# A channel-product weight scheme moved one batch earlier, with filled waits in the first attention: a three-layer mixer on one Trainium2 core

## The chip, the cores and the metric

The kernel runs on one core of one Trainium2 chip. The metric is the time of one execution on the device in microseconds; the profile is one such execution with every instruction recorded. The engines are PE (TensorE: matmuls, with PEld for its weight loads), DVE (VectorE), ACT (ScalarE), POOL (GpSimd) and SP (SyncE, which here only issues DMAs).

## What is computed

Eight batches of 576 tokens with 512 features pass through a chunked attention (8 heads of 64, chunks of 64 tokens), a token and channel mixer with ReLU, and a gated unit with a spatial product:

```python
# attention, per batch, head and chunk of 64 tokens
p = exp(s - max(s)); attn = p / (sum(p) + 1e-9)      # s = q k^T / 8
x = attn @ v                                          # (8, 576, 512)
# mixer
u = x + (relu(x^T @ w_tok1) @ w_tok2)^T               # 576 -> 256 -> 576
x = u + relu(u @ w_ch1) @ w_ch2                       # 512 -> 1536 -> 512
# gated unit
h = relu(x @ w_in)                                    # 512 -> 1024, halves g and v
v_n = (v - mean(v)) / sqrt(var(v) + 1e-6)
out = (g * (w_spatial @ v_n + b)) @ w_out             # 512 -> 512
```

All inputs and the output are float32; q and k are scaled so that the scores spread widely.

## The kernel before

Each float32 operand is held as two float16 parts (hi and lo), and a product is three float16 matmuls (hi·hi, hi·lo, lo·hi), 288 or 512 columns wide. The work runs batch by batch. In a batch PE goes through the first channel product (`ch1`), the second (`ch2`), the first token product of the next batch (`tok1`), the gate products (`gate_v`, `gate`), the second token product of the next batch (`tok2`), the spatial product (`gated`), and the output products (`proj`), four or five of which are left for the next batch. Batches are counted from 0.

From some batch on the two channel products are formed from seven products of quarter blocks in place of eight (`ch1_fast` at line 750, `ch2_fast` at line 834). They need sums of weight blocks, which `sum_steps` (line 665) makes once: `join` adds the two parts on DVE (L683) and, for each block that is used as it is, issues DMAs to a buffer in HBM (L687, L691); `first` and `second` are four sums on POOL (L695, L696, L699, L700); `high` splits on ACT (L703), `low` on DVE (L706), and its DMAs (L708, L713) store the result. Before, the first channel product is formed so from batch 2 on (`FIRST_FAST = 2`) and the second from batch 3 on (`FIRST_FULL = 3`): the sums for the first are made in batch 1 and those for the second in batch 2, while batch 2 runs the full `ch2` (L921, 288 matmuls). `ch1_fast(full)` stores its result either as it is (`store`, when the second product is still full) or as the seven block sums that `ch2_fast` needs (`sums_of`).

Attention for batch b+1 runs in batch b, in tiles of 128 tokens. Batches 0 and 1 have `wide_steps` (line 343, float32 matmuls on PE); batch 0's stands alone at the start of the program, in the order of the list `FIRST_ORDER` (sc score, sh maximum, ex exponentials, nm division, tn transposes on PE, tu their copy, at the product with v, oh and ol the split), with the first weight splits (U, L, H, O) between. From the attention for batch 2 on, `at_steps` (line 225) has each tile's steps at the places `TIMES` (line 426): load of q and k at 0, score at 10.9, `p_lo` on POOL at 17.2, `p_turn` (a transposing DMA, L281) at 18, `attend` (L298) at 23.7, `x_turn` (the next transposing DMA, L320) at 27.2.

What sets the order. PE's instructions stand in the order in which the program is written. `pump` (line 467) advances a clock by each matmul's columns, and `tick` calls what is due by it: attention steps, weight sums, and operations that `after` put off by one of `LAGS`. `PACES` scales the attention's clock by stage, `SPAN` its length. From batch 2 on ACT, DVE, POOL and SP are in written order too (`manual_schedule`, `exact`); in batches 0 and 1 a scheduler chooses their order. `bank()` hands out four PSUM tiles in turn; a product waits for its tile to be emptied.

## Time and profile before

| what | value |
|---|---|
| median of 3 runs | 1127.51 us (1127.5 to 1128.74) |
| the profiled execution's own time | 1132.01 us |
| its span, first to last instruction | 1130.2 us |
| PE busy | 1084.3 us (96%) |
| DVE, ACT, POOL busy | 773.1, 515.2, 436.6 us |
| granted TensorE clock, mean | 0.994 of full |

The span begins with the first instruction. A busy PE is not PE at its peak: matmuls overlap each other, so their rate is read from the starts of following groups. A view by stretch of time shows how much of a stretch each engine works, and a timeline shows the idle time before a row and what ended it.

### The profile page before, as it was taken

To read this page: it belongs to the slowest core of one execution; us is meant where nothing else is said; L and a number is where in the kernel's file an instruction comes from. 1 tells how busy PE (TensorE), PEld (TensorE's weight loads), DVE (VectorE), ACT (ScalarE), POOL (GpSimd) and SP (SyncE) were. 2 spreads that over 40 slices of the span, in tenths; PEclk is the share of its full clock that TensorE was granted. 3 is DMA by queue.
4 is the path that set the end of the run, shared out by engine and by line. 5 is a ranking of instruction groups with operands and counts; after the bars stand their busy time and mean duration, and the time that the engine had idled before them with its cause. 6 is when DMAs were issued, how large, how long until landed. Compare 5 with 4: busy or idle time off the path is not lost.

```text
span 1130.2 us, 26065 instructions
## 1 busy us (share of the span) xinstructions
PE 1084.3 (96%) x10860; PEld 771.6 (68%) x10860; DVE 773.1 (68%) x1301; ACT 515.2 (46%) x1040; POOL 436.6 (39%) x416
## 2 busy tenths in 40 slices
PE   5898999999999899999999999999999999999998
PEld 4577757776676675776667666777767767677765
DVE  4899977665455677878577676877768774577342
ACT  6455543434335445456254652556344652346131
POOL 0000032534244464656235551375435551255221
PEclk9899999999999999999999999999999999999999
DMA  9478620454027675255931678245931666024401
GB/s 325 138 236 269 198 75 20 127 146 113 6 54 217 160 135 119 54 158 163 249 76 47 175 181 189 51 117 164 238 89 36 172 166 190 1 66 147 134 1 47
DMA packets 147270, 148.31 MB, mean 131 GB/s; under 512 B 95824, under 2 KB 108112, under 8 KB 144848
## 3 DMA queue, kind: packets, MB, share of 16 engines
q1 hardware_dynamic: 147152, 146.64, 47.9%
q8 instruction: 85, 1.39, 0.5%
q14 instruction: 33, 0.27, 0.1%
HBM read 112.00 MB, written 20.45 MB: 117 GB/s over the span
## 4 chain that ended last, share of the span: by engine, by line
PE 72%; DVE 13%; ACT 5%; DMA 3%; POOL 3%; issue 3%; SPq 0%; DVEq 0%; ACTq 0%; POOLq 0%
PE mp L735 22%; PE mp L499 21%; PE mp L921 8%; PE mp L947 7%; PE mp L1035 7%; PE mp L522 3%; DVE gb L155 1%; PE mp L246 1%; ACT inw L377 1%; DMA pT<-p 1%; PE mp L298 1%; DVE gb L159 1%; DMA x<-xht 1%; DVE c L803 1%; DVE hb L624 1%
## 5 line engine op out<-in xcount | busy, mean ns | idle before, releaser
L735 PEld LDWEIGHTS <-c1w 128*128 128x128 f16 x2772 | 269.0, 98 | 80.2 <-issue 7.6
L735 PE MATMUL mp<-xb,c1w 128*128 128x288 f16 x864 | 129.1, 286 | 4.2 <-DVE vn L797 2.6
L921 PE MATMUL mp<-hb,c2w 128*128 128x288 f16 x864 | 111.6, 289 | 0.0
L499 PE MATMUL mp<-spw,vn 128*128 128x288 f16 x896 | 111.2, 286 | 0.1
L499 PEld LDWEIGHTS <-vn 128*128 128x128 f16 x896 | 87.6, 98 | 22.6 <-issue 0.3
L499 PE MATMUL mp<-xb,inw 128*128 128x288 f16 x768 | 100.2, 286 | 0.1
L921 PEld LDWEIGHTS <-c2w 128*128 128x128 f16 x864 | 83.8, 99 | 22.1
L1035 PE MATMUL mp<-otw,gb 128*128 128x512 f16 x432 | 98.1, 379 | 0.0
L735 PE MATMUL mp<-hb,c1w 128*128 128x288 f16 x630 | 90.4, 286 | 2.0 <-ACT vn L863 1.9
L499 PEld LDWEIGHTS <-inw 128*128 128x128 f16 x768 | 74.3, 98 | 23.5 <-issue 0.3
L735 PE MATMUL mp<-c2w,c1w 128*128 128x288 f16 x630 | 89.7, 286 | 0.0
L947 PE MATMUL mp<-inw,xb 128*128 128x512 f16 x384 | 87.3, 379 | 0.8 <-DVE x L416 0.8
L499 PE MATMUL mp<-xb,c1w 128*128 128x288 f16 x576 | 73.4, 286 | 4.9 <-DVE xb L583 2.5
L1035 PEld LDWEIGHTS <-gb 128*128 128x128 f16 x432 | 42.3, 98 | 45.4
L1023 POOL TENSOR_TENSOR gb<-gt,gb 128x576 f16<-128x576 f32 x31 | 43.3, 1402 | 69.6 <-ACT gb L1022 69.6
L499 PEld LDWEIGHTS <-c1w 128*128 128x128 f16 x576 | 55.7, 98 | 20.1 <-issue 5.0
L947 PEld LDWEIGHTS <-xb 128*128 128x128 f16 x384 | 37.4, 98 | 43.3 <-issue 1.0
L970 POOL TENSOR_TENSOR y<-z,mhalf 128x1 f32<-128x1 f32 (+1 forms) x40 | 25.7, 643 | 104.3 <-DVE z L969 104.3
L735 PE MATMUL mp<-c1w 128*128 128x288 f16 x432 | 64.7, 286 | 0.0
L981 POOL TENSOR_TENSOR vn<-vt,vn 128x512 f16<-128x512 f32 x32 | 37.8, 1181 | 57.3 <-ACT vn L980 57.3
L695 POOL TENSOR_TENSOR xs<-xs 128x128 f32<-128x128 f32 x12 | 8.7, 724 | 115.4 <-DVE xs L683 115.4
L499 PE MATMUL mp<-t2w,hb 128*128 128x288 f16 x384 | 49.1, 286 | 1.8 <-ACT hb L1013 0.8
(231 smaller groups left out, 2035.5 us busy)
## 6 DMA issues: line engine op xcount, KB each, us to landing
c1w<-c2s SPq DMA_DIRECT2D x70, 384.0 KB, 3.6
c1w<-c1s SPq DMA_DIRECT2D x72, 256.0 KB, 3.3
qk<-in_qk SPq DMA_DIRECT2D x49, 256.0 KB, 4.3
c1w<-c1s SPq DMA_DIRECT2D x32, 384.0 KB, 3.3
out<-o SPq DMA_DIRECT2D x31, 256.0 KB, 2.3
v<-in_v SPq DMA_DIRECT2D x56, 128.0 KB, 4.1
vn<-in_wc SPq DMA_DIRECT2D x4, 1024.0 KB, 6.7
otw<-in_wc SPq DMA_DIRECT2D x3, 1024.0 KB, 5.2
```

The costliest lines, as they stand in the source:

```text
L155: DVE.scalar_tensor_tensor(out=t, in0=w[:, :, 1], scalar=0xC0000000, in1=t, op0=ALU.bitwise_and, op1=ALU.bitwise_or)
L159: DVE.scalar_tensor_tensor(out=t, in0=w[:, :, 0], scalar=29, in1=t, op0=ALU.logical_shift_right, op1=ALU.bitwise_or)
L246: PE.matmul(out=sp[t, r, 64 * h:64 * h + 64], lhsT=qk16[half[r], x, 0, h, t], rhs=qk16[half[r], y, 1, h, t], start=(k == 0), stop=(k == 2))
L499: PE.matmul(out=o, lhsT=l, rhs=r, start=(i == 0), stop=(i == len(seq) - 1))
L522: PE.matmul(out=pss[m], lhsT=l, rhs=r, start=(i + j == 0), stop=False)
L735: PE.matmul(out=o[:, 0:288], lhsT=w[:, a, k], rhs=b(e, k), start=(start and k + i == 0), stop=(stop and k == 1 and i == 2), skip_group_che ...
L921: PE.matmul(out=o, lhsT=c2w[:, a, k, mc], rhs=hb[:, k // 2, r, k % 2 * 2 + t], start=(k + e == 0), stop=(k == 11 and e == 2))
L947: PE.matmul(out=ps, lhsT=l, rhs=r, start=(k + e == 0), stop=(k == 3 and e == len(seq) - 1))
L970: POOL.tensor_tensor(out=y[0:n], in0=z[0:n], in1=mhalf[0:n], op=ALU.pow)
L981: POOL.tensor_tensor(out=vn[:, 2 * j + 1], in0=t, in1=vn[:, 2 * j], op=ALU.subtract)
L1023: eng.tensor_tensor(out=gl, in0=t, in1=gh, op=ALU.subtract)
L1035: PE.matmul(out=ps, lhsT=gb[:, l, k, tk], rhs=otw[:, r, k], start=(k == 0 and e == 0), stop=(k == 3 and e == 2))
```

## The change

1. `FIRST_FULL` goes from 3 to 2: batch 2 forms the second channel product by `ch2_fast` (252 matmuls of 288 columns in place of 288), and its `ch1_fast` stores the block sums. All weight sums are made in batch 1, those for the second product (12 rounds of `sum_steps`) beside those for the first (6 rounds). Each pair of rounds uses the two halves of its room in turn.
2. ACT, DVE, POOL and SP stand in written order from batch 1 on. `LAGS` has three more entries (two for `residual`, one for `ch1`), and the one for `put` in `ch2_fast` goes from 0 to 0.4.
3. In batch 1 the two output products that are left over run before `tok2` and no longer after it.
4. In the attention steps of `at_steps`, `p_turn` moves to 19.2, `attend` to 24.6, the load of v behind the maximum, `x_lo` a little ahead. Paces and spans for batches 1 and 2 change.
5. In the first attentions, tiles 1 and 3 of batch 0 take the exponential in one ACT instruction after a subtraction on DVE, with the sum by a DVE reduction, where the others use eight ACT instructions with a bias and an accumulator. Ahead of five groups of transposes or products with v, and of the first `ch1` of batch 0, PE gets matmuls of 256 columns whose result is overwritten (`fill`, 35 and 12).

```diff
-    FIRST_FAST, FIRST_FULL = 2, 3
+    FIRST_FAST, FIRST_FULL = 2, 2
...
+    def fill(o, n):
+        for _ in range(n):
+            PE.matmul(out=o, lhsT=gall[:, 4608:4736], rhs=gall[:, 4608:4608 + o.shape[-1]], start=True, stop=True, skip_group_check=True)
...
+    INSIDE = (0, 2, 4, 5, 6, 7, 8, 9)
+    FILL_TURN, FILL_ATTEND = {3: 4, 4: 8}, {2: 4, 3: 14, 4: 5}
...
-            DVE.tensor_scalar(out=mx[rows], in0=mx[rows], scalar1=-0.125, scalar2=None, op0=ALU.mult)
+            if inside:
+                DVE.tensor_scalar(out=mx[rows], in0=mx[rows], scalar1=-0.125, scalar2=None, op0=ALU.mult)
+            else:
+                DVE.tensor_tensor(out=m["sd"][rows].rearrange("p h r k -> p r h k"), in0=sc,
+                                  in1=mx[rows].to_broadcast([n, 2, 4, 64]), op=ALU.subtract)
 
         def expo():
+            if not inside:
+                ACT.activation(out=m["sd"][rows], in_=m["sd"][rows], func=AF.Exp, scale=0.125)
+                return
...
-    TIMES = [0, 7, 8.2, 10.9, 11, 11.5, 12.1, 13.2, 14.6, 14.8, 16.2, 17.2, 18, 18.1, 19.6, 23.7, 25.1, 26, 27.2]
+    TIMES = [0, 7, 8.2, 10.9, 11.5, 11.7, 12.1, 13.2, 14.6, 14.8, 16.2, 17.2, 18.1, 19.2, 19.6, 24.6, 25.1, 25.8, 27.2]
...
-    BEHIND = {10.9: (8.2, 500.0), 23.7: (18, 5300.0)}
+    BEHIND = {10.9: (8.2, 500.0), 24.6: (19.2, 5300.0)}
...
+    SPAN0, SUMS = 105000.0, (2000.0, 1150.0)
...
-            f = rv[:, 0:512].rearrange("p (k m) -> p k m", k=2)
-            s = rv[:, 512:1024].rearrange("p (n m) -> p n m", n=4)
-            g = rv[:, 0:512].bitcast(F16).rearrange("p (n e m) -> p n e m", n=4, e=2)
+            here, there = [rv[:, 512 * i:512 * i + 512] for i in (q, 1 - q)]
+            f = here.rearrange("p (k m) -> p k m", k=2)
+            s = there.rearrange("p (n m) -> p n m", n=4)
+            g = here.bitcast(F16).rearrange("p (n e m) -> p n e m", n=4, e=2)
...
-            if b == FIRST_FAST:
+            if b == FIRST_FAST - 1:
                 ordered.enter_context(tc.manual_schedule(engines={ET.Activation, ET.DVE, ET.Pool, ET.SP}))
                 exact[0] = True
-                sum_pump([(2, p, q) for p in range(6) for q in range(2)], 1550.0)
-            if b == FIRST_FAST - 1:
-                sum_pump([(1, p, None) for p in range(6)], 2200.0)
+                sum_pump(1, [(p, None) for p in range(6)], SUMS[0])
+                sum_pump(2, [(p, q) for p in range(6) for q in range(2)], SUMS[1])
...
+                if b == FIRST_FAST - 1:
+                    for i in pend:
+                        proj(b - 1, i)
+                    pend = []
```

Three places show what moves; the rows are instructions in program order, without times. The first is DVE at the start of the program, from the second tile's maximum to the third's (mp is a PSUM tile, inw the room of the scores). Before:

```order
L370 TENSOR_REDUCE mx<-mp 128x8
L371 TENSOR_SCALAR mx<-mx 128x8
L383 TENSOR_SCALAR total<-total 128x8
L384 RECIPROCAL total<-total 128x8
L385 TENSOR_TENSOR inw<-inw,total 128x512
```

Now:

```order
L378 TENSOR_REDUCE mx<-mp 128x8
L382 TENSOR_TENSOR inw<-mp,mx 128x2x4x64
L402 TENSOR_SCALAR total<-total 128x8
L403 RECIPROCAL total<-total 128x8
L404 TENSOR_TENSOR inw<-inw,total 128x512
L401 TENSOR_REDUCE mx<-inw 128x8
```

The small scaling is now a subtraction of a whole tile, and a reduction (L401) stands ahead of the division; ACT has one exponential there in place of eight.

The second is ACT at the start of batch 1's first channel product (L623, now L649, empties a product's PSUM tile; L703, now L731, is `high` of a weight sum, vn for the first product, xs for the second). Before:

```order
L703 ACTIVATE vn<-vn 128x4x256
L623 ACTIVATE hb<-mp 128x576 x2
L234 ACTIVATE qk_86<-qk_85 128x1024
L623 ACTIVATE hb<-mp 128x576
L703 ACTIVATE vn<-vn 128x4x256
```

Now:

```order
L238 ACTIVATE qk_86<-qk_85 128x1024
L731 ACTIVATE xs<-xs 128x4x128
L649 ACTIVATE hb<-mp 128x576
L731 ACTIVATE vn<-vn 128x4x256
L649 ACTIVATE hb<-mp 128x576
L731 ACTIVATE xs<-xs 128x4x128
L649 ACTIVATE hb<-mp 128x576
```

Between almost every two PSUM tiles that ACT empties there is now a split that waits for POOL.

The third is ACT at the start of batch 2's first channel product (L796, now L820, copies a partial product; L1022, now L1046, belongs to the spatial product of batch 1). Before:

```order
L796 ACTIVATE vn<-mp 128x288
L1022 ACTIVATE gb<-gt 128x576
L764 ACTIVATE vn<-vn 128x288
L556 ACTIVATE hb<-vn 128x288
L822 ACTIVATE hb<-mp 128x288
L703 ACTIVATE xs<-xs 128x4x128
```

Now:

```order
L820 ACTIVATE vn<-mp 128x288
L840 ACTIVATE xs<-xs 128x288
L1046 ACTIVATE gb<-gt 128x576
L846 ACTIVATE hb<-mp 128x288
L848 ACTIVATE xs<-mp 128x288
```

The weight sum's split is gone, and the steps are those of the batches that form both products from seven.

## Rows read from the trace of the kernel before

**Rows 1.** The page, part 1: busy time and share of the span by engine.

```profile
PE 1084.3 (96%) x10860; PEld 771.6 (68%) x10860; DVE 773.1 (68%) x1301; ACT 515.2 (46%) x1040; POOL 436.6 (39%) x416
```

**Rows 2.** Busy by stretch: length, PE, PEld, DVE, ACT, POOL, clock, DMA, GB/s.

```profile
54.00:140.70 86.70, 82.45 (x979) 64.93 (x977) 85.24 (x112) 46.20 (x126) 4.55 (x3) 1.00 0.72 227
194.33:331.33 137.00, 136.68 (x1398) 97.80 (x1396) 81.13 (x128) 54.37 (x88) 59.27 (x58) 1.00 0.32 87
744.98:880.00 135.02, 133.13 (x1371) 95.29 (x1369) 98.53 (x172) 65.77 (x125) 62.85 (x56) 1.00 0.53 140
```

**Rows 3.** The same view: batches 2 and 4, each in three parts.

```profile
331.33:377.08 45.75, 44.59 (x362) 30.89 (x360) 23.60 (x42) 21.45 (x44) 20.24 (x30) 1.00 0.73 197
377.08:423.49 46.41, 42.64 (x674) 32.48 (x672) 34.06 (x48) 21.37 (x36) 28.09 (x31) 0.96 0.67 138
423.49:476.45 52.96, 51.21 (x446) 34.01 (x437) 43.37 (x75) 24.72 (x43) 26.81 (x30) 1.00 0.38 85
611.52:655.95 44.43, 44.43 (x362) 30.90 (x360) 30.15 (x53) 26.36 (x53) 24.36 (x19) 1.00 0.58 163
655.95:693.04 37.09, 34.24 (x447) 26.62 (x444) 25.62 (x43) 15.12 (x28) 15.81 (x15) 1.00 0.93 209
693.04:744.98 51.94, 51.94 (x534) 34.81 (x532) 40.08 (x72) 24.16 (x42) 20.54 (x19) 1.00 0.25 61
```

**Rows 4.** Timeline of PE in batch 4's second product: start, length, what.

```profile
655.95 1.27 PE L735 MATMUL mp<-hb,c1w 128*128 128x288 f16 x9
657.05 1.27 PE L735 MATMUL mp<-c2w,c1w 128*128 128x288 f16 x9
```

**Rows 5.** Waits in batch 2, 331 to 476: total us, times, longest.

```profile
ACT xs L703 <- POOL xs L700: 27.6, 11, 3.9
DVE xs L683 <- DMA c2s<-xs: 8.6, 6, 2.6
```

**Rows 6.** Busy in batch 2 on the tile xs alone: DVE, ACT, POOL.

```profile
331.33:476.45 145.12, 17.15 (x23) 7.54 (x12) 27.29 (x46) 0.99 0.59 137
```

**Rows 7.** Lines 687 and 713: DMA issues on SP, ns min/median/max, starts.

```profile
L687 SPq DMA_DIRECT2D c1s<-c1w x36: 359/468/2090, 46.3 to 99.4; - x36
...
L713 SPq DMA_DIRECT2D c2s<-xs x24: 359/371/719, 339.9 to 461.1; - x24
```

**Rows 8.** Groups by line: batch 1, then batch 2, of DVE's line 237.

```profile
L237 DVE TENSOR_TENSOR qk<-qk,qk 128x1024 f16<-128x1024 f32 x3 | 4.1, 1382 | 0.0
...
L237 DVE TENSOR_TENSOR qk<-qk,qk 128x1024 f16<-128x1024 f32 x6 | 9.9, 1658 | 2.1 <-ACT qk L234 2.1
```

**Rows 9.** Timeline of PE, start of the program and batch 2's token product.

```profile
28.79 0.47 PE L401 MATMUL mp<-pT,hb 64*64 64x64 f32 x2 [2.88 <-ACT pT L393]
...
34.25 7.38 PE L522 MATMUL mp<-x,t1w 128*128 128x512 f16 x24
...
53.41 4.92 PE L499 MATMUL mp<-xb,c1w 128*128 128x288 f16 x38 [2.30 <-DVE xb L583]
...
423.49 5.36 PE L522 MATMUL mp<-x,t1w 128*128 128x512 f16 x24
```

**Rows 10.** Busy by stretch, as rows 2: a stretch of the first attention.

```profile
27.70:37.90 10.20, 8.64 (x109) 5.91 (x110) 8.49 (x15) 5.41 (x14) 0.00 (x0) 0.52 0.47 166
```

**Rows 11.** Timeline of DVE in the same part.

```profile
33.67 0.69 DVE L416 SCALAR_TENSOR_TENSOR x<-mp,x 128x512 f16<-128x512 f32 x1 [1.33 <-ACT xT L411]
...
39.12 0.76 DVE L168 SCALAR_TENSOR_TENSOR t2w<-gb,t2w 128x576 f16<-128x576 f32 x1 [0.75 <-ACT t2w L165]
...
42.73 1.29 DVE L530 SCALAR_TENSOR_TENSOR hb<-mp,hb 128x512 f16<-128x512 f32 x2 [0.99 <-ACT hb L529]
```

**Rows 12.** Busy of ACT's line 377 alone, tiles 0 and 1 of batch 0.

```profile
8.18:12.81 4.63, 4.63 (x32) 1.00 1.09 256
```

**Rows 13.** Groups by line: busy us, mean ns, then idle before.

```profile
L260 ACT ACTIVATE sd<-sd 128x512 f32<-128x512 f32 (+1 forms) x30 | 18.7, 624 | 17.9 <-DVE sd L256 17.9
```

**Rows 14.** Tile pT, batches 3 to 6: what its readers waited for, us, times.

```profile
  DMA pT<-p: 2.4, 3
```

More of the change, by code (lines that the diff above doesn't have):

```diff
@@ L381, in norm @@
             sd = m["sd"][rows].rearrange("p h r k -> p (h r) k")
-            mx = m["sum"].rearrange("p h r e -> p (h r) e")
+            if inside:
+                mx = m["sum"].rearrange("p h r e -> p (h r) e")
+            else:
+                mx = sm.tile([128, H, 1], F32, name="mx")
+                DVE.tensor_reduce(out=mx[rows], in_=sd, axis=AX.X, op=ALU.add)
             DVE.tensor_scalar(out=mx[rows], in0=mx[rows], scalar1=1e-9, scalar2=None, op0=ALU.add)
@@ L713, in low, with sum_pump, sum_end @@
                     SP.dma_start(out=c2s[q, 3:7, :, at + e * 256:at + e * 256 + 128].rearrange("n p m -> p n m"), in_=g[:, :, e])
[L715 to L730 removed]
+        return [join, first, second, high, low] + [lambda: None] * (2 if stage > 1 else 0)
+    todo_sums = {1: [], 2: []}
+    def sum_pump(stage, what, gap):
+        todo = todo_sums[stage]
+        todo.extend(f for w in what for f in sum_steps(stage, *w))
+        pumps.append([clock[0], gap, lambda: todo.pop(0)(), lambda: len(todo) > 0, clock])
+    def sum_end(stage):
+        while todo_sums[stage]:
+            todo_sums[stage].pop(0)()
     def fast_product(o, w, b, start, stop, whole=True):
@@ L1097, in when @@
                     return max(base + (at[1] - first) * unit, slow[0] + (at[1] - at[0]) * unit * 0.6)
-                pumps.append([base, span / (end - todo[0]) if b < 3 else when, a_step, lambda: todo[0] < end and a_open(), slow])
+                pumps.append([base, span / (end - todo[0]) if b < 2 else when, a_step, lambda: todo[0] < end and a_open(), slow])
         def held_tick():
```

65 lines of the change are left out of this document (31 added, 34 removed).

## The prediction

> **What bounds the kernel now.** I read the shares by engine first: PE is busy 96% of the span [rows 1], so a gain comes either from fewer matmuls or from the few places where PE stands. The busy time by stretch says where those are. Batch 1 has PE at 136.68 of 137.00 us, a later batch with both products in seven parts (batch 5) at 133.13 of 135.02 [rows 2]. Batch 2, the one in between, is the slow one: its three parts take 45.75, 46.41 and 52.96 us, 145.12 in all, where the same parts of batch 4 take 44.43, 37.09 and 51.94, 133.46 in all [rows 3]. Both have five output products in the first part and five tiles of attention, so they differ only in the second channel product and in the weight sums that batch 2 carries. Before batch 0 ends the bound is another: from 54 to 140.7 us DVE works 85.24 of 86.70 us [rows 2] on splitting the weights, so a time gained or lost ahead of that stretch on DVE is carried through it.
>
> **The change, part by part.**
>
> *Batch 2.* 36 matmuls of 288 columns go. In a stretch without holes nine of them pass in 657.05 − 655.95 = 1.10 us, 0.122 each [rows 4], so 36 are 4.4 us. That is less than half of the 9.3 us by which the middle part is longer than batch 4's (46.41 − 37.09) [rows 3]. The other 4.9 are stalls. In that batch ACT stands 27.6 us in front of the split of a weight sum because POOL has not finished it, and DVE 8.6 us for the DMA that must leave the room before the next sum [rows 5]; all that follows on these in-order engines, the exponentials and the splits of q and k among them, is late by it. The sums are gone from batch 2 with the change (17.15 us of DVE, 7.54 of ACT, 27.29 of POOL [rows 6]), while `ch1_fast` gets the block sums of the later batches; that is batch 4's program. I take batch 4's time: −11.7 us (145.12 − 133.46). The bounds: if no wait goes, −4.4; if batch 2 ran at batch 4's PE busy time, 44.43 + 34.24 + 51.94 = 130.6 [rows 3], −14.5.
>
> *Batch 1.* It takes those sums: DVE goes from 81.13 to 98.3 us of some 137, ACT from 54.37 to 61.9, POOL from 59.27 to 86.6 [rows 2, 6]. PE's work is the same. SP gets 24 issues for the split sums, 30 for blocks of the second product's weights and 30 for those of the first that so far went out in batch 0 (six of each stay there): 60 × 0.468 + 24 × 0.371 = 37 us of SP's time [rows 7], ahead of or between the transposing DMAs and the loads of q, k and v, which wait behind them on the same queue. No engine is full. What it costs PE is read from batches with as much DVE work in written order: batch 5 has 98.53 us of it and leaves PE 135.02 − 133.13 = 1.9 us without work, batch 2, with sums, 145.12 − (44.59 + 42.64 + 51.21) = 6.7, batch 1 so far 0.3 [rows 2, 3]. So the cost lies between −0.3 and +6.4. I take batch 5's, +1.6: the load is the same, the dense products of batch 1 need only their PSUM tile emptied and have four of them, and with two halves of the room in turn the next `join` no longer waits for the DMA; that wait passes to POOL's first sum of the next round, several steps after the DMA was issued. The two output products that move ahead of `tok2` are the same work at another place: nothing.
>
> *The first attention.* Eight exponentials with their accumulators take ACT 4.63 / 2 = 2.3 us a tile [rows 12]; one over the whole tile takes 0.62 [rows 13]. For two tiles that is 3.4 us off ACT, and on DVE a subtraction and a reduction of a whole tile, 0.69 each as its other operations of that size [rows 11], in place of a small one, some 1.2 us a tile, which fit into holes that DVE has in the first 28 us. ACT's later work moves ahead by 0.5 to 2 us. I walk it to the first product of tile 3 with v, 28.79 [rows 9] to some 28.3, and to the token product, 34.25 to some 33.1, behind 13 fills (256 columns, 0.11 us each by the rate of rows 4) that stand ahead of tile 4's transposes and product, of which about 1 us is on the way. The clock is the larger part: between 27.7 and 37.9 it was granted at 0.52 [rows 10], level 1.2 GHz, while PE stood 2.88 us ahead of tile 3's product [rows 9]; the 24 token matmuls take 7.38 us there and 5.36 in batch 2 [rows 9]. With 18 fills around that hole I expect full clock, and the token product done near 39.2 in place of some 42 (34.25 + 7.38 and four more matmuls). What then ends last is DVE: between 28.5 and 42.7 us it has holes of 1.33, 0.75 and 0.99 us [rows 11]. The second stays (ACT's split of a weight), of the first about 0.4 is left, the third goes: with a small shift before them −2.2 us when the split of the token product begins. The 12 fills ahead of the first channel product, 1.3 us, lie in a hole of 2.30 [rows 9] that DVE ends. As DVE is full up to 140 us, the 2.2 us are kept; bounds −3.1 (all three holes) and +1 (nothing gained, the fills of tile 4 paid). If the cover of the 12 fills were gone they would cost 1.3.
>
> *Later batches.* `attend` now stands 7.4 units behind `p_lo` in place of 6.5, `p_turn` 2.0 in place of 0.8, so SP stands less in front of its transposing DMA. PE's waits for that tile were 2.4 us in batches 3 to 6 [rows 14]. I take half, −1.2; bounds −2.4 and, as the last tile of a batch now ends nearer to `tok1`, as much the other way, +2.4. The later `put` and residuals (0.4 and 0.5 us) stand behind matmuls that don't read them at once: nothing, covered by the product that follows.
>
> **The sum:** −2.2 + 1.6 − 11.7 − 1.2 = −13.5 us. It is made in the profiled execution of 1132.0, so 1118.5 there; that execution lies 4.5 over the median of 1127.5, and I set the same difference against the median: 1114.0.
>
> **A rule against it.** DVE's split of q and k took 1.38 us a time in batch 1 and 1.66 in batch 2, where POOL did more [rows 8]: the two slow each other. The Trainium skill ("SBUF — State Buffer", section "Who interferes with whom") says that a DVE instruction with two inputs in SBUF and a POOL instruction that reads SBUF exclude each other for a whole instruction. The trace agrees in direction; by that rule each of POOL's added sums could hold one DVE instruction of batch 1, and the rival on batch 1 below would be the likelier one. From the rows: 27.29 us more on DVE's 98.3 is 126 of 137, still not full.
>
> **Rivals.**
> 1. *Batch 2 keeps its stalls.* They would then come from the attention for batch 3, whose exponentials, splits and transposes stand in the same queues, and not from the sums. For it: batch 4 also has 37.09 − 34.24 = 2.9 us without PE work in its middle part [rows 3]. Against it: ACT's 27.6 us behind POOL [rows 5] have no counterpart once the sums are gone. Only the 4.4 us of products are won: −2.2 + 1.6 − 4.4 − 1.2 = −6.2, 1121.3. Chance 0.18.
> 2. *Batch 1 becomes bound by ACT behind POOL.* Each `high` stands in ACT's queue ahead of the operation that empties the next PSUM tile, and waits for POOL; 27.6 / 11 = 2.5 us each in batch 2, 3.9 at most [rows 5]. Batch 1 has 18 of them: at 2.5 us ACT is at 62 + 45 = 107 of 137. It decides from (137 − 62) / 18 = 4.2 us a wait. At 5.5 it is 62 + 99 = 161 us, 24 over the 137 of now, and the kernel is at 1127.5 − 13.5 − 1.6 + 24 = 1136.4, slower than before. Chance of slower 0.04; of a cost near 15 us that leaves no difference 0.03; of 6 to 12 us, near 1122, 0.05.
> 3. *The fills don't hold the clock.* Then the token product still takes 7.4 us and ends near 41.7; the third hole shrinks to 0.5 and only about 0.7 us is won at the start: 1115.5. For it: the fills fill 2 of the 3 us of that hole, and PE stands some 2 us behind them. Chance 0.15.
>
> **How the numbers follow.** The forecast has 0.55, the rivals 0.18, 0.12 and 0.15. A difference under 0.2% (2.3 us) is about what a measurement of this kernel can't tell from none. Faster by more: 0.55 + 0.18 + 0.15 + 0.05 = 0.93; within it 0.03; slower 0.04. The range: the best ends of all terms are −3.1 − 0.3 − 14.5 − 2.4 = −20.3, 1107.2; above, it takes in rival 1 at 1121.3. So 1107 to 1121.5.
>
> **What would show it.** Right: the stretch from batch 2's first block product to batch 3's lasts near 133.5 us, its middle part near 37; batch 1 stays under 140, with ACT's waits for POOL's sums now there, about 2.5 us each; the granted clock is full from 20 to 54 us; DVE's split of the token product begins near 40.5. Wrong: a middle part of batch 2 over 40 us (rival 1); a batch 1 over 145 with PE waiting for ACT or DVE at its PSUM tiles (rival 2); a granted clock near 0.5 around the first token product (rival 3). A total under 1107 would say that the written order of batch 1 also removes holes that I don't see, one over 1121.5 that a wait has moved and not gone.

## The result, and the profile after

The changed kernel takes 1138.17 us (median of 5 runs, 1136.44 to 1140.16) against 1128.74 (1127.5 to 1131.9) for the kernel before in the same session: a ratio of 1.0077, with 1.0055 to 1.01 as its 95% interval. It is slower by 0.8%, where 1114.0 and faster was forecast. The profiled execution of before, 1132.01 us, is slower than all five of these runs, that of after, 1136.48, is 1.7 under its median; so the two spans, 1130.2 and 1134.7 us, differ by 4.5 us where the medians differ by 9.4. The account below is that of the 4.5.

The page's first part, after, answers to [rows 1]:

```profile
PE 1087.6 (96%) x10871; PEld 773.4 (68%) x10871; DVE 802.5 (71%) x1337; ACT 520.8 (46%) x1026; POOL 447.8 (39%) x424
```

PE is busy 3.3 us more. 36 products less (−4.4) and 47 fills more (47 × 0.11 = 5.2) make 0.8 of it; the rest is mostly work at a lower clock. Busy by stretch, after (length, PE, PEld, DVE, ACT, POOL, clock, DMA, GB/s): batch 1, its first channel product, the rest of it up to the token product, and its tail; then batch 2 in the three parts of [rows 3].

```profile
191.86:344.81 152.95, 143.42 (x1494) 100.97 (x1492) 113.71 (x160) 63.46 (x103) 86.25 (x105) 0.97 0.57 140
191.86:228.98 37.12, 37.12 (x434) 29.33 (x432) 31.25 (x38) 17.45 (x28) 25.84 (x34) 1.00 0.58 146
228.98:313.38 84.40, 74.87 (x803) 50.51 (x801) 58.00 (x89) 34.11 (x56) 45.99 (x61) 0.94 0.70 170
313.38:344.81 31.43, 31.43 (x262) 21.13 (x260) 24.46 (x35) 11.90 (x21) 14.41 (x11) 1.00 0.20 51
344.81:389.25 44.44, 44.44 (x363) 30.93 (x361) 29.88 (x56) 26.42 (x54) 20.97 (x17) 1.00 0.49 146
389.25:433.35 44.10, 36.58 (x590) 28.07 (x588) 32.52 (x52) 18.75 (x34) 19.48 (x17) 0.98 0.99 233
433.35:486.45 53.10, 53.10 (x443) 34.67 (x437) 38.15 (x68) 24.86 (x43) 22.99 (x20) 0.95 0.24 52
```

The same middle stretch of batch 1 before:

```profile
231.45:299.84 68.39, 68.39 (x754) 47.89 (x752) 40.53 (x77) 27.47 (x45) 30.62 (x31) 1.00 0.39 101
```

So the account in the two profiles, by PE's starts: batch 1 begins 2.47 us earlier (194.33 before, 191.86 after); it lasts 152.95 in place of 137.00 [rows 2], +15.95; batch 2 lasts 141.64 in place of 145.12, −3.48; all that follows 1134.7 − 486.45 = 648.25 in place of 1130.2 − 476.45 = 653.75, −5.5. That makes +4.5. Batch 1 loses all of it in the middle stretch, which grows from 68.39 to 84.40 us. PE's timeline there (start, length, what, and in brackets the idle time before it and what ended it):

```profile
236.99 0.22 PE L250 MATMUL mp<-qk 64*64 64x64 f16 x4 [1.97 <-ACT qk L238]
238.88 0.54 PE L250 MATMUL mp<-qk 64*64 64x64 f16 x44 [1.66 <-DVE qk L241]
239.35 5.64 PE L945 MATMUL mp<-hb,c2w 128*128 128x288 f16 x31
...
253.41 0.54 PE L250 MATMUL mp<-qk 64*64 64x64 f16 x44 [1.04 <-DVE qk L241]
253.88 3.97 PE L945 MATMUL mp<-hb,c2w 128*128 128x288 f16 x31
259.71 0.57 PE L302 MATMUL mp<-pT,v 64*64 64x64 f16 x48 [1.85 <-DMA pT<-p]
...
281.56 0.22 PE L250 MATMUL mp<-qk 64*64 64x64 f16 x4 [0.87 <-ACT qk L238]
283.70 0.54 PE L250 MATMUL mp<-qk 64*64 64x64 f16 x44 [1.92 <-DVE qk L241]
```

PE stands 1.97 + 1.66 + 1.04 + 1.85 + 0.87 + 1.92 = 9.3 us, at the scores (L250) for the splits of q and k, once for a transposed tile. It doesn't stand at the PSUM tiles of the dense products. Behind three of these stops the clock falls: 31 products at 239.35 take 5.64 us, where 31 at full clock, at 253.88, take 3.97. The clock in three short windows:

```profile
239.30:243.00 3.70, 3.70 (x34) 2.52 (x22) 3.15 (x5) 0.48 (x1) 1.65 (x4) 0.62 1.06 264
259.50:263.50 4.00, 3.79 (x64) 2.65 (x65) 3.08 (x6) 2.41 (x5) 3.58 (x4) 0.65 0.53 128
284.00:288.00 4.00, 4.00 (x41) 1.56 (x29) 3.34 (x7) 1.49 (x3) 1.36 (x4) 0.57 0.86 212
```

By the rows it costs 5.64 − 3.97 = 1.7 us at the first; at the second 54 products take 8.46 us (260.21) where 54 at full clock take 6.79 (245.43), again 1.7; at the third 15 output products take 5.10 us (284.18), where 24 at full clock take 5.34 (319.42), so 15 some 3.4, and it is 1.7 once more. That makes some 5 us, an estimate. Two groups of scores that lay elsewhere before (96 instructions more) add about 1. Time without work is 152.95 − 143.42 = 9.5 us, where before it was 0.3. Together that is some 15 of the 16 us.

Why q and k are late is seen on ACT (timeline, after):

```profile
229.18 0.65 ACT L649 ACTIVATE hb<-mp 128x576 f16<-128x576 f32 x1
233.90 0.63 ACT L731 ACTIVATE xs<-xs 128x512 f16<-128x512 f32 x1 [4.07 <-POOL xs L728]
234.43 1.04 ACT L731 ACTIVATE vn<-vn 128x1024 f16<-128x1024 f32 x1
235.38 0.61 ACT L279 ACTIVATE p<-sd 128x512 f16<-128x512 f32 x1
235.90 1.04 ACT L238 ACTIVATE qk<-qk 128x1024 f16<-128x1024 f32 x1
```

ACT stands 4.07 us in front of the split of a weight sum, then does the split for the other product, then p, then q and k, whose load was issued by 222.1 us; the median load of q and k lands 4.3 us after its issue. PE has wanted them since 235. The Trainium skill ("PSUM — Partial Sum Buffer", section "Engine vs sequencer instructions") says that the queues of these engines are strict FIFO; these rows agree. ACT's waits in batch 1, after (total us, times, longest):

```profile
ACT xs L731 <- POOL xs L728: 20.6, 6, 4.9
...
ACT vn L731 <- POOL vn L728: 5.2, 3, 2.7
```

In batch 2 the waits of [rows 5] are gone, and still the middle part takes 44.10 us in place of the 37 forecast. Its timeline on PE:

```profile
412.47 0.57 PE L302 MATMUL mp<-pT,v 64*64 64x64 f16 x48 [1.83 <-DVE mx L269]
...
428.52 0.22 PE L250 MATMUL mp<-qk 64*64 64x64 f16 x4 [1.28 <-ACT qk L238]
429.88 0.54 PE L250 MATMUL mp<-qk 64*64 64x64 f16 x44 [1.14 <-DVE qk L241]
432.89 0.53 PE L302 MATMUL mp<-pT,v 64*64 64x64 f16 x24 [2.47 <-ACT sd L264]
433.35 1.46 PE L544 MATMUL mp<-x,t1w 128*128 128x512 f16 x3
```

It is the attention: the scores of the next batch's first tile (428.52), and the exponential and the product with v of the last tile (432.89, 24 matmuls for 64 tokens), all stand directly ahead of the token product (L544).

### The profile page after: what moved, and what is told of

The parts are those of the page before. It is cut to its first block, busy times and chain, and to the rows that moved or that the text cites. A ratio compares the mean times of both kernels' runs of the same rounds, so it can differ in the third digit from the quotient of the medians.

```text
span 1134.7 us, 26167 instructions
## 1 busy us (share of the span) xinstructions
PE 1087.6 (96%) x10871; PEld 773.4 (68%) x10871; DVE 802.5 (71%) x1337; ACT 520.8 (46%) x1026; POOL 447.8 (39%) x424
## 4 chain that ended last, share of the span: by engine, by line
PE 73%; DVE 12%; ACT 4%; DMA 4%; issue 3%; SPq 2%; POOL 2%; DVEq 0%; ACTq 0%; POOLq 0%
PE mp L759 25%; PE mp L521 22%; PE mp L971 9%; PE mp L1059 7%; PE mp L544 3%; PE mp L945 3%; DVE gb L155 1%; DVE gb L159 1%; DMA pT<-p 1%; PE mp L250 1%; DVE hb L650 1%; PE mp L302 1%; DMA hb<-in_qk 1%; SPq L719 1%; DVE c L827 1%
## 5 line engine op out<-in xcount | busy, mean ns | idle before, releaser
L759 PEld LDWEIGHTS <-c1w 128*128 128x128 f16 x3024 | 293.2, 98 | 82.0 <-issue 3.2
L759 PE MATMUL mp<-hb,c1w 128*128 128x288 f16 x756 | 108.6, 286 | 0.9 <-ACT vn L887 0.7
L759 PE MATMUL mp<-c2w,c1w 128*128 128x288 f16 x756 | 107.9, 286 | 0.0
L945 PE MATMUL mp<-hb,c2w 128*128 128x288 f16 x576 | 77.0, 294 | 1.7 <-ACT sd L392 1.7
L945 PEld LDWEIGHTS <-c2w 128*128 128x128 f16 x576 | 56.8, 100 | 17.9 <-issue 1.9
L521 PEld LDWEIGHTS <-c1w 128*128 128x128 f16 x576 | 55.7, 98 | 15.5 <-DVE c1w L168 0.9
L613 POOL TENSOR_TENSOR xb<-rt,xb 128x576 f16<-128x576 f32 x4 | 6.3, 1568 | 138.2 <-ACT xb L612 138.2
L580 POOL TENSOR_TENSOR hb<-t,hb 128x576 f16<-128x576 f32 x36 | 48.6, 1369 | 19.5 <-ACT hb L579 19.5
```

Of the source, the lines that this page charges most:

```text
L521: PE.matmul(out=o, lhsT=l, rhs=r, start=(i == 0), stop=(i == len(seq) - 1))
L580: eng.tensor_tensor(out=lo, in0=t, in1=hi, op=ALU.subtract)
L759: PE.matmul(out=o[:, 0:288], lhsT=w[:, a, k], rhs=b(e, k), start=(start and k + i == 0), stop=(stop and k == 1 and i == 2), skip_group_che ...
L945: PE.matmul(out=o, lhsT=c2w[:, a, k, mc], rhs=hb[:, k // 2, r, k % 2 * 2 + t], start=(k + e == 0), stop=(k == 11 and e == 2))
```

## The experiments

Each line below was run beside the kernel before; "batch 1" and "batch 2" are PE's time from a batch's first channel product to the next one's, in the profiled execution, so each is one execution's. In e2 to e6, e8, e9, e11, e15, e16 and e18 batch 2 has the code of after; it took 141.64 to 142.06 us in after and in all of these but e15 (142.55) and e3 (143.56), so differences of a few us in these columns can be read.

| run | against before, 95% | batch 1 | batch 2 |
|---|---|---|---|
| changed kernel | 1.0077 [1.0055, 1.01] | 152.95 | 141.64 |
| e1 sums2_later | 0.9939 [0.9923, 0.9956] | 137.55 | 143.32 |
| e2 sched_b1 | 1.0168 [1.0153, 1.0183] | 162.73 | 141.92 |
| e3 blocks_early | 1.006 [1.0043, 1.0077] | 150.17 | 143.56 |
| e4 high_late | 1.0159 [1.0135, 1.0183] | 163.78 | 141.93 |
| e5 spread | 1.0041 [1.0022, 1.0059] | 147.47 | 141.75 |
| e6 third_room | 1.0043 [1.003, 1.0055] | 150.12 | 141.89 |
| e7 first_attention | 0.9984 [0.9973, 0.9995] | 137.00 | 145.35 |
| e8 late_scores | 1.0077 [1.0054, 1.0099] | 152.17 | 141.66 |
| e9 sums_from_batch0 | 1.0087 [1.0054, 1.0119] | 146.23 | 141.64 |
| e10 pace_batch2 | 1.0054 [1.004, 1.0069] | 159.54 | 131.16 |
| e11 sums_on_dve | 1.0109 [1.0086, 1.0132] | 155.15 | 142.06 |
| e12 one_after_other | 1.0191 [1.0169, 1.0213] | 154.68 | 153.25 |
| e13 one_after_other_paced | 1.0169 [1.0144, 1.0194] | 161.25 | 143.46 |
| e14 and_blocks_early | 1.0183 [1.0159, 1.0207] | 158.62 | 145.53 |
| e15 second_half_out | 1.0033 [1.0018, 1.0048] | 147.91 | 142.55 |
| e16 first_half_out | 1.0031 [1.0015, 1.0047] | 145.90 | 141.66 |
| e17 later_and_paced | 0.9953 [0.9937, 0.9969] | 144.30 | 139.12 |
| e18 dve_relieved | 1.0109 [1.0086, 1.0132] | 155.67 | 142.06 |

### Which part of the change costs it: e1, e2, e7

e1 puts the second product's sums back into batch 2:

```diff
-    FIRST_FAST, FIRST_FULL = 2, 2
+    FIRST_FAST, FIRST_FULL = 2, 3
...
-                sum_pump(2, [(p, q) for p in range(6) for q in range(2)], SUMS[1])
+            if b == FIRST_FULL - 1:
+                sum_pump(2, [(p, q) for p in range(6) for q in range(2)], 1330.0)
...
```

> The changed kernel with the weight sums of the second channel product made in batch 2 again, where that product is again the full one (as before the change); written order from batch 1, the sums of the first product and the first attention stay as changed. The changed kernel's batch 1 took 152.95 us from its first channel product to batch 2's first block product (137.00 before). Theory A (ACT and DVE stand in written order behind POOL's sums for the second product, and the splits of q and k behind them reach PE late): without these sums batch 1 is at 137 to 140 us, and batch 2 back at about 145; in all near 1127. Theory B (SP's issues of weight blocks and stores hold the transposing DMAs and the loads): half of the blocks stay, so batch 1 is half way, 144 to 147, in all 1131 to 1134. Theory C (the written order in batch 1 costs this by itself): batch 1 stays at 148 or more, in all 1135 or more.

1121.61 us against 1128.76: theory A's 137 to 140 for batch 1 came true, its total of 1127 was 5 too high. Batch 1 of e1 in the view by stretch:

```profile
190.83:328.38 137.55, 137.55 (x1494) 98.73 (x1492) 93.39 (x136) 57.66 (x91) 57.79 (x57) 1.00 0.48 121
```

No time without work, full clock. The written order in batch 1, the first product's sums and their block stores cost nothing; theory C falls. ACT there splits q and k at 230.16, 5.7 us earlier than in after, 4.7 of it counted from the start of the batch (its timeline in e1):

```profile
228.15 0.65 ACT L649 ACTIVATE hb<-mp 128x576 f16<-128x576 f32 x1 [0.22 <-PE mp L521]
228.70 1.05 ACT L731 ACTIVATE vn<-vn 128x1024 f16<-128x1024 f32 x1
229.64 0.62 ACT L279 ACTIVATE p<-sd 128x512 f16<-128x512 f32 x1
230.16 1.05 ACT L238 ACTIVATE qk<-qk 128x1024 f16<-128x1024 f32 x1
```

What makes after slow is the second product's sums in batch 1, with the stores of blocks that go with them. e1 also beats the kernel before, by 0.6%, and no run here was faster. By the two profiles (1130.2 and 1119.0 us) it gains 3.5 us at the start, loses 0.55 in batch 1, gains 1.8 in batch 2 and 6.5 behind it.

e2 has the scheduler's order in batch 1, all sums still there:

```diff
...
-            if b == FIRST_FAST - 1:
+            if b == FIRST_FAST:
                 ordered.enter_context(tc.manual_schedule(engines={ET.Activation, ET.DVE, ET.Pool, ET.SP}))
```

> The changed kernel with ACT, DVE, POOL and SP of batch 1 in the scheduler's order as before, written order from batch 2 on; all weight sums stay in batch 1. Theory A: no engine's queue stands behind a sum that isn't ready unless the scheduler puts it there; batch 1 near 138 to 143, in all 1123 to 1128. Theory B: the same 60 block issues lie in batch 1, so 146 or more, in all 1131 or more. Theory C: as A, batch 1 below 140.

Batch 1 takes 162.73 us, ten more than in written order. A and C missed; the number fits B's open figure of 146 or more, of which e3 below leaves 2.8 us. With these sums there, the written order is no cause but a help.

The kernel before with the first attention alone (the diff of the change's fifth point):

> The kernel before with the changed first attention alone (two tiles with one exponential, 35 fills there and 12 ahead of the first channel product); nothing else is changed. The prediction's term: 2.2 us less when batch 1 begins (bounds 3.1 less and 1 more), so near 1126.5 against 1128.7, the clock full from 20 to 54 us. Rival: the fills don't hold the clock or DVE's other waits take the place, 0 to 0.7 us less, 1128 to 1128.7.

1127.16 against 1129.47, a ratio of 0.9984; batch 1 begins at 192.33 in place of 194.33. The prediction's first term holds. The clock was not full throughout, though; after, in two windows:

```profile
28.00:41.70 13.70, 11.75 (x148) 6.87 (x145) 11.52 (x19) 7.02 (x15) 0.00 (x0) 1.00 0.61 208
41.70:45.00 3.30, 2.88 (x13) 1.88 (x14) 2.92 (x5) 1.06 (x1) 0.00 (x0) 0.58 0.99 278
```

### Which queue holds the splits: e3, e4, e5, e6, e11, e18, e8

e3 issues the stores of unchanged blocks in batch 0:

```diff
-        def join():
-            DVE.tensor_tensor(out=f, in0=w[:, 0], in1=w[:, 1], op=ALU.add)
+        def blocks():
...
+                with tc.issue_after(mark):
+                    for p in range(6):
+                        sum_steps(1, p, None, True)
+                        sum_steps(2, p, 0, True)
```

> The changed kernel with the DMAs that store unchanged weight blocks (36 for the first product, 36 for the second) issued in batch 0, once the weights are split, and no longer with the sums in batch 1. Only SP's queue is lighter in batch 1, by some 30 us of issue time. Theory A: PE's waits at the scores stay; batch 1 at 149 or more, in all 1134 or more. Theory B: the stores of sums and the transposes go out at once, POOL's sums start on time, batch 1 at 139 to 143, in all 1124 to 1129.

Batch 1 is 2.8 us shorter and batch 2 1.9 longer. Theory A's figures came true, B's did not: SP's issues of blocks are a small part. The part can be seen: the wait of 1.85 us for a transposed tile, at 259.71 in after, has no counterpart in e3.

e4 has the split two steps later:

```diff
-        return [join, first, second, high, low] + [lambda: None] * (2 if stage > 1 else 0)
+        idle = lambda: None
+        return [join, first, second, idle, idle, high, low] if stage > 1 else [join, first, second, idle, high, low]
```

> The changed kernel with ACT's split of a weight sum placed later in the written order: two empty steps (2.3 us) behind POOL's last sum for the second product, in place of the two at the end of a round, and one (2.0 us) for the first. Theory A in its narrow form (ACT stands behind POOL because its split is written too early, 20.6 us in six waits of up to 4.9): these waits fall below 8 us, PE's waits at the scores shrink, batch 1 at 141 to 146, in all 1127 to 1132. Theory B: POOL is late because the store of the round before holds the room; the later place of the split delays that store too, batch 1 stays at 150 to 156, in all 1135 to 1141.

The waits at the first scores go, ACT's wait for POOL's sums falls only to 13.1 us in five, and batch 1 is 10.8 us longer, past both theories' figures: PE now stands for transposed tiles (waits of e4 from 192 to 300):

```profile
ACT xs L731 <- POOL xs L728: 13.1, 5, 4.5
PE mp L302 <- DMA pT<-p: 12.9, 3, 5.4
```

e5 calls the sums more slowly (`SUMS` 1150.0 becomes 1500.0), e6 gives them a third part of a room:

```diff
-            here, there = [rv[:, 512 * i:512 * i + 512] for i in (q, 1 - q)]
+            third = tq4.rearrange("p a b c -> p (a b c)").bitcast(F32)
+            here, there = [(rv[:, 0:512], rv[:, 512:1024], third[:, 0:512])[(2 * p + q + i) % 3] for i in range(2)]
```

> The changed kernel with the sums for the second product called every 1.5 us of PE's clock in place of 1.15, so 12 rounds of seven steps take 126 us in place of 97. Theory D (a round is a chain through two half rooms that cross: join on DVE, four sums on POOL, the split on ACT and DVE, the store and its landing, and only then POOL's first sum of the next round; some 1.8 + 0.6 + 0.7 + 1.0 + 3.0 = 7 us and each engine's queue, against 8.05 us a round): at 10.5 us a round the chain has 3.4 us to spare, the waits mostly go, batch 1 at 139 to 144, in all 1124 to 1130. Theory E (the sums' work itself is too much beside the second product and the attention, whatever the room): the same work reaches into the gate and the token stretch, batch 1 at 146 to 152, in all 1131 to 1138.

> The changed kernel with three parts of a room for the sums of the second product, taken in turn (the third lies in a tile that is unused until the end of batch 1), so a round's first sum no longer waits for the store of the round just before; pace, order and work are the same. Theory D: POOL's waits for the store (10.0 us in four) go, ACT's behind POOL fall below 10 us, batch 1 at 140 to 145, in all 1125 to 1131. Theory E: batch 1 stays at 149 or more, in all 1134 or more.

147.47 and 150.12, in all 1133.93 and 1134.13: both are theory E's figures, and D's were missed. In e6 ACT stands 16.3 us behind POOL's sums where after has 20.6, and PE's first two waits at the scores are nearly the same, 1.84 and 1.66 us. The room is part of the wait, not its root.

e11 moves the four sums of a round from POOL to DVE; e18 moves its `join` and `low` from DVE to POOL:

```diff
+        eng = POOL if stage == 1 else DVE
...
-            POOL.tensor_tensor(out=s[:, 2], in0=a21, in1=a22, op=ALU.add)
...
+            eng.tensor_tensor(out=s[:, 2], in0=a21, in1=a22, op=ALU.add)
...
```

> The changed kernel with the four sums of each round for the second product on DVE and no longer on POOL. DVE gets 48 operations of 128x128, at 0.2 to 0.25 us about 11 us more of some 137; POOL 22 us less. Theory A or D (engines wait for each other in the chain of a round, ACT for POOL above all): ACT's waits for POOL's sums vanish, batch 1 at 141 to 147, in all 1127 to 1133. Theory E with DVE as the engine that doesn't keep up: batch 1 at 155 or more, in all 1140 or more.

> The changed kernel with join and low of each round for the second product on POOL and no longer on DVE: 24 operations less on DVE (21.5 us in batch 1), so DVE's work there is that of the kernel with these sums in batch 2; POOL gets some 30 us more (86 to about 116). A round then has no DVE in it. Theory I (DVE is the full engine: in the 9.6 us ahead of PE's first wait at the scores it is busy 9.49, in the kernel with the sums in batch 2 7.74 of 9.59 at the same place): batch 1 at 140 to 146, in all 1125 to 1132. Theory A or E (the round's chain through POOL and ACT is what the attention stands behind): with 30 us more on POOL batch 1 is at 151 to 158, in all 1136 to 1143.

155.15 and 155.67: in e11 the figure for DVE as the engine that doesn't keep up, in e18 that of theories A and E. With no such sum left on POOL ACT waits 4.79 us at the same split, for DVE; with nothing of a round left on DVE it waits 5.67, for POOL (ACT's timeline in e11, then in e18):

```profile
235.88 0.63 ACT L733 ACTIVATE xs<-xs 128x512 f16<-128x512 f32 x1 [4.79 <-issue]
```

```profile
235.50 0.63 ACT L731 ACTIVATE xs<-xs 128x512 f16<-128x512 f32 x1 [5.67 <-POOL xs L728]
```

The split of q and k begins at 237.88 and 237.50, in after at 235.90. So taking work off one of these two engines and putting it on the other only moves the wait there. (In e11 the releaser is not told by the row; DVE's last sum of the round, L730, runs from 235.50 to 235.79.) Theory I, that DVE alone is the full engine, falls with e18, although DVE is nearly without a pause ahead of the first wait. After, and e1 at the same place:

```profile
223.40:232.99 9.59, 9.59 (x123) 7.56 (x122) 9.49 (x14) 3.88 (x7) 4.98 (x9) 1.00 0.66 169
```

```profile
222.37:231.96 9.59, 9.59 (x123) 7.56 (x122) 7.74 (x11) 5.95 (x9) 5.69 (x6) 1.00 0.60 154
```

In after DVE has a share in ACT's wait of 4.07 us. POOL had stood for 4.46 us ahead of it, and goes on just behind DVE's `join` (L711) of a round for the first product; the sum that ACT waits for is the last of the eight that POOL then does, four of each stream (DVE's and POOL's timelines; the row names another releaser that ended 0.12 us before, and the data come from the `join`):

```profile
227.01 1.21 DVE L711 TENSOR_TENSOR vn<-c1w 128x1024 f32<-128x1024 f16 x1
228.41 0.72 POOL L723 TENSOR_TENSOR vn<-vn 128x256 f32<-128x256 f32 x1 [4.46 <-ACT hb L649]
233.41 0.46 POOL L728 TENSOR_TENSOR xs<-xs 128x128 f32<-128x128 f32 x1
```

e8 has PE read the scores and the product with v later:

```diff
         s0, gap = BEHIND[s]
+        if g < 3 * NT:
+            gap += 3500.0
```

> The changed kernel, where in batch 1 alone PE reads the scores' operands 3.5 us later in its order behind their splits, and the product with v 3.5 us later behind its transposing DMA (the rest of the attention moves along). Theory F (the queues are late by a few us but keep up: ACT's and DVE's splits of q and k come 1 to 3 us after PE wants them): the waits at the scores and at v in the second product go, the clock stays full, batch 1 at 139 to 144, in all 1125 to 1130. Theory E (ACT, DVE and POOL don't keep up with this much work in that stretch): the lateness grows with the delay, batch 1 at 149 or more, in all 1134 or more.

152.17, theory E's figure: nothing gained. The first wait shrinks from 1.97 to 0.72 us, one of 3.41 us appears ahead of a product with v (297.08).

### Where the sums stand: e9, e12, e15, e16

e9 begins the second product's sums in batch 0, behind its `ch2`:

```diff
...
-                sum_pump(2, [(p, q) for p in range(6) for q in range(2)], SUMS[1])
...
                 mark = last[-1]
+                sum_pump(2, [(p, q) for p in range(6) for q in range(2)], SUMS[1])
                 pumps.append([clock[0], 4000.0, held_tick, lambda: wdone[0] < len(W), clock])
```

> The changed kernel with the sums for the second product begun in batch 0, behind its second channel product (some 52 us ahead of batch 1, where POOL is busy 14 and ACT 19 of 52 us), at the same pace: six to seven of the twelve rounds are done when batch 1 begins, the rest in its first channel product, none beside its second. Theories A, D, E and F alike: without sums for the second product beside that product its stalls go, batch 1 at 137 to 141; batch 0's tail grows by 0 to 3 us; in all 1122 to 1128. If the stalls come from elsewhere (the first product's sums, the paces, the order): batch 1 stays at 147 or more, in all 1132 or more.

Both figures for batch 1 were missed; the total is 1138.11 us. Batch 1 is 6.7 us shorter, and PE's last wait in it ends at 251 us, but it begins at 200.60, 8.7 later. PE waits in batch 0's `tok2`:

```profile
178.26 1.14 PE L521 MATMUL mp<-t2w,hb 128*128 128x288 f16 x4 [5.47 <-ACT hb L551]
```

e12 runs the first product's sums first (1450.0 in place of 2000.0 a step), the second's behind them:

```diff
...
-        pumps.append([clock[0], gap, lambda: todo.pop(0)(), lambda: len(todo) > 0, clock])
+        pumps.append([clock[0] + (stage - 1) * 30 * SUMS[0], gap, lambda: todo.pop(0)(), lambda: len(todo) > 0, clock])
```

> The changed kernel with the sums for the first product done first (a step every 1.45 us in place of 2.0, so six rounds take 43.5 us, about the length of batch 1's first channel product), and those for the second behind them at the old pace; the work is the same. Theory H (the two streams of sums run at once, and where both fall between two steps of the attention, DVE does two joins and two splits, POOL eight sums and ACT two splits ahead of the splits of q and k, which come late by as much; one stream at a time fits, as in the kernel with the second product's sums in batch 2): batch 1 at 138 to 143, in all 1123 to 1129. Theory E (the work beside the second product is too much in any order): batch 1 at 148 or more, in all 1133 or more.

154.68: theory H falls. The scores still wait 2.5 us twice beside the second product (0.19 + 2.33 at 240, 0.60 + 1.93 at 255), and the sums now reach into batch 2, where SP's last stores are still going out at 352 us and PE stands 8.55 us:

```profile
358.72 2.56 PE L759 MATMUL mp<-xb,c1w 128*128 128x288 f16 x10 [8.55 <-DVE vn L821]
```

e15 leaves out rounds 7 to 12, e16 rounds 1 to 6; the stores of unchanged blocks stay in batch 1 in both:

```diff
...
+        if stage == 2 and 2 * p + q >= 6:
+            return [blocks] + [lambda: None] * 6
...
```

> The changed kernel with rounds 7 to 12 of the sums for the second product left out (their join, sums, splits and stores; plain weight blocks are stored in their place in batch 0, so the output is another). Those are the rounds that run from 240 us on, beside the second channel product and the gate; rounds 1 to 6 stay beside the first. Batch 1 took 152.95 us with twelve and 137.55 with none. If each stall belongs to the sums that run at that moment (theory E, local): only the first waits, around 234 to 237 us, stay, 4 us with the clock's share, batch 1 at 140 to 143, in all 1125 to 1129. If the lateness is carried on by the attention once it has arisen: batch 1 at 146 or more, in all 1131 or more.

> The other half: rounds 1 to 6 left out (again with plain blocks stored in batch 0 in their place, so the output is another), rounds 7 to 12 stay, from 240 us on. Theory E, local: the waits around 234 to 237 us go, those from 250 us on stay, batch 1 at 144 to 150, in all 1130 to 1135. If the lateness arises in the first channel product and is only carried on: batch 1 at 137 to 141, in all 1122 to 1127.

e16 came out at its local figures, e15 at those of a lateness carried on. Over the 137.55 us of e1, rounds 1 to 6 with all block stores cost 10.4, rounds 7 to 12 with all of them 8.4, all twelve 15.4. Yet the waits lie where the sums run. In e15:

```profile
235.79 0.22 PE L250 MATMUL mp<-qk 64*64 64x64 f16 x4 [1.96 <-ACT qk L238]
237.68 0.54 PE L250 MATMUL mp<-qk 64*64 64x64 f16 x44 [1.66 <-DVE qk L241]
251.50 0.54 PE L250 MATMUL mp<-qk 64*64 64x64 f16 x44 [0.33 <-DVE qk L241]
258.50 0.57 PE L302 MATMUL mp<-pT,v 64*64 64x64 f16 x48 [2.55 <-DMA pT<-p]
```

In e16:

```profile
251.61 0.57 PE L302 MATMUL mp<-pT,v 64*64 64x64 f16 x48 [1.15 <-DMA pT<-p]
265.10 0.57 PE L302 MATMUL mp<-pT,v 64*64 64x64 f16 x48 [1.71 <-DMA pT<-p]
273.89 0.22 PE L250 MATMUL mp<-qk 64*64 64x64 f16 x4 [1.39 <-ACT qk L238]
```

Without the early rounds the pair of waits at 236 to 238 us is gone; without the late ones those from 265 us on are. The wait at 258 in e15 comes 18 us behind its last round, but is not lateness carried on: POOL has p done at 250.4, and SP issues six stores of unchanged blocks, which the edit leaves in place, ahead of the transposing DMA (SP's timeline in e15):

```profile
250.46 4.72 SPq L718 DMA_DIRECT2D c2s<-c2w  x6
255.29 1.25 SPq L285 DMA_TRANSPOSE pT<-p  x1
```

The first wait in e16 stands behind such stores too (six from 244.10, the transposing DMA at 247.82, p done at 244.3), and so does the one at 259.71 in after.

### Batch 2 and the combinations: e10, e17, e13, e14

e10 has other paces for the attention in batch 2:

```diff
-             {"first": 0.0, "pair": 1.15, "ch1": 0.95, "ch2": 1.7, "gate": 1.15, "tok1": 1.0, "last": 0.2, "turn": 0.9},
+             {"first": 0.3, "pair": 1.15, "ch1": 0.95, "ch2": 1.7, "gate": 1.15, "tok1": 1.0, "last": 1.4, "turn": 0.5},
```

> The changed kernel with other paces for the attention in batch 2 only: its second tile's scores move ahead of batch 2, so three groups of scores and not four lie in its second channel product. Theory G (batch 2 is long because the attention for batch 3 begins only behind batch 1's token product, 32 us ahead of batch 2, where later batches have 52, and is pressed into the second product): batch 2's middle part falls from 44.1 to 38 to 41 us, its end too, in all 3 to 6 us less than the changed kernel, 1132 to 1135. Rival: the middle part stays over 43 us, because the splits of the second product's own results hold the queues.

Batch 2 falls to 131.16 us, its middle part from 44.10 to 35.91:

```profile
394.80:430.71 35.91, 34.67 (x495) 26.82 (x493) 26.74 (x45) 15.79 (x29) 18.31 (x16) 1.00 0.96 235
```

Theory G holds, and by more than I had put. But batch 1, into whose tail the scores moved, grows by 6.6 (2.33 and 1.27 us of waits at them). About 3 us are left by the medians (1135.02), and the two intervals overlap.

> The kernel with the second product's sums in batch 2 (that run: 1121.6, batch 1 137.55, batch 2 143.32) and the attention's paces for batch 2 of the run on them, which move the second tile's scores into batch 1's tail, where now no sum runs. Theory G: one group of scores less beside the second product, batch 2 at 136 to 141, batch 1 longer by 0 to 3, in all 1116 to 1121. Rival: batch 2's waits come from its own sums now, no change beyond 1 us.

The same paces in e1: batch 2 gains 4.2, batch 1 loses 6.75 where I had 0 to 3, and the median is 1123.45, no better than e1's. The scores in the tail wait as in e10 (2.33 us at 330.31, 1.27 at 331.80), with no sum beside them.

> The kernel of the run before, with the attention's paces for batch 2 as in the run on them (the second tile's scores ahead of batch 2's block products). That run had batch 2 at 131.2 in place of 141.6, and batch 1 longer by 6.6, since the sums were still going there. Theory H with G: batch 2 at 131 to 134, batch 1 at 140 to 147, 3 to 7 us less than the run before, in all 1117 to 1125. If the scores in batch 1's tail cost what they save: within 2 us of the run before.

> The kernel of the run before, with the stores of unchanged weight blocks issued in batch 0. Alone that took 2.8 us off the changed kernel's batch 1 and nothing off its median that a measurement tells. If the queue of SP is what is left, 1 to 3 us less than the run before; if it was hidden behind the other waits, within 1 us of it.

e13 is e12 with `"first": 1.6`, `"last": 1.15` and `"turn": 0.5` in the paces, e14 is e13 with e3's diff. Both have e12's sums that reach into batch 2, and both keep that wait (8.58 and 10.07 us at its block products): 1147.5 and 1149.65 us. All figures put down for the two were missed.

## Why the prediction was wrong, by its own steps

**Batch 1, +1.6 (bounds −0.3 and +6.4): +15.95.** This is the larger of the two steps that failed; batch 2 is the other. I read "no engine is full" and took the cost from batch 5, because the load was the same, and I looked for a wait at the PSUM tiles of the dense products. Those have four tiles and never waited. The attention for batch 2 has no such cover. Its splits of q and k, p and its transposes stand in the same in-order queues as the rounds of sums, each a chain over DVE, POOL, ACT, DVE and SP, and PE reads the result of a split at a fixed place in its own order. e1 shows that these sums, with their block stores, are the cause; e15 and e16 that half of the rounds with all block stores costs more than half; e3, e5 and e6 that SP's issues of blocks, the pace and the room carry 2.8, 5.5 and 2.8 us when eased alone; e11 and e18 that moving the work between DVE and POOL doesn't help. Batch 5 has as much DVE work, but nothing in it is a sum ahead of the attention's splits. How the 16 us divide among the queues stays open: the waits change place with each edit, and no edit that kept the twelve rounds in batch 1 brought it under 147 us.

Rival 2 named the queue (ACT's splits of sums, waiting for POOL), and the total came out near its 1136.4. That is luck: it has 24 us on batch 1 and batch 2's whole gain, where 16 and little gain were measured. Its mechanism was another: ACT full and the PSUM tiles late. ACT waits 20.6 + 5.2 = 25.8 us for POOL's sums in nine waits, 2.9 each, well under the 4.2 from which I let it decide, and with 63 us of work it is far from full. The wait of 4.07 us cost PE 1.97 + 1.66, because the operation behind it is one that PE is about to read, and the fallen clock behind such waits adds some 5 over the batch.

**DVE in batch 1** works 113.71 us, not 98.3, so the load was not batch 5's either: it is 93.39 in e1 without the sums, 12.3 over the 81.13 from which I started, and 20.3 come with them where I had 17.15. Its L241 took 1.85 us at 236.97, while POOL's L282 ran from 236.07 for 1.67, and 1.21 at 252.15, where POOL was idle until 253.08. The Trainium skill ("SBUF — State Buffer", section "Who interferes with whom") says that a DVE instruction with two inputs in SBUF and a POOL instruction that reads SBUF exclude each other; the trace agrees in direction, 0.64 us here. No run takes this out alone, so its part in the 16 us is not shown.

**Batch 2, −11.7: −3.48.** This step failed too. Rival 1 came true, for the reason it gave: e10 shows that the place of the attention sets this time. "That is batch 4's program; I take batch 4's time" was wrong, since the attention's place differs: behind batch 1's token product there are 31 us up to batch 2 (313.38 to 344.81), behind batch 3's 52 (565.05 to 616.99). So 590 instructions of PE lie in the middle part where batch 4 had 447 [rows 3], with the same 252 products of blocks. The sums' waits of [rows 5] went, the time hardly did. My own rows could have told: before, the middle part of batch 2 had 674 instructions of PE and batch 4's 447 [rows 3], and the 36 products explain only 36 of these 227. e10 has batch 2 at 131.16, below the 133.5 that I had expected, paid for elsewhere.

**Start, −2.2: −2.47 in the profile of after, −2.0 in e7's.** With the fills the clock held over the token product (24 matmuls in 5.35 us, before 7.38 [rows 9]; no run has them without the other exponentials); DVE's split of it began at 41.38, in e7 at 40.94, not 40.5 (before 42.73). That −2.47 lies so near is in part luck: behind this split the clock fell in both executions. Where it stayed full, in e8 and e10, which have after's code up to there, batch 1 begins at 190.98 and 190.80, 3.4 and 3.5 us earlier than in the profile of before and past the best bound of −3.1.

**Later batches, −1.2: −5.5 in the two profiles.** The direction was right, the place was not. Batch 3 has 4.5 of it: 135.07 us before, 130.54 after, and 130.5 to 130.7 in every run that forms both products of batch 2 from seven. PE's time without work there falls from 5.3 to 1.5 us; before, 3.1 of it were waits for DVE in the block products and 1.6 for another transposing DMA, and only 0.5 the wait for pT that I had counted on. Two executions of code that is the same from batch 3 on (before and e7) differ by 3.3 us (653.75 and 650.4), so the size of the rest is not settled; e1 has 647.3.

## What to carry to other kernels

Side work on a filled set of in-order engines isn't costed by an engine's free share: list the operations that the bound engine reads at a fixed place, and see what stands ahead of each in its queue and what that waits for. A batch with the same program is no price for another batch when work from its neighbour is placed differently; compare what lies in each stretch first, by the instruction counts too. And when a change has several parts, run it with each part undone: here one part left in its old place turned a loss of 0.8% into a gain of 0.6%.

## What the runs showed of the hardware that was not expected

In after the clock fell behind short waits in the midst of dense work: PE stood for 3.6 of 3.9 us (235.0 to 238.9), and the stretch behind had 0.62 on average, part of it at 1.2 and part at 2.4 GHz, with products 0.18 us apart in place of 0.12 (31 in 5.64 us). It fell behind the wait of 1.85 us ahead of 259.71 too, and stayed full behind that of 1.04 us ahead of 253.41. In batch 0, code that is the same began the first channel product at 48.2 to 48.6 us in most executions and at 50.1 to 50.5 in four (after, e7, e12, e17); in after's the clock was 0.58 from 41.7 to 45.0, in e1's full, with the same two waits of PE ahead of it (0.26 and 1.54 us, from 39.7 to 42.1 in after).
